# Two products that add to the same PSUM columns, with another block's product between them

## The chip, the cores and the metric

The kernel runs on one core of one Trainium2 chip. The metric is the device time of one execution in microseconds; lower is better. The program is written in Tile: the code says what depends on what, and a scheduler at build time sets the order in which each engine gets its instructions.

## The reference, cut to what matters

A causal attention with a bias from cumulative sums is followed by a gated feed-forward part. B = 8 batches, H = 8 heads, S = 576 tokens, D = 64, 512 model columns, 1024 feed-forward columns, all float32.

```
scores = (q @ k.T) / 8                                  # 64 heads of 576 x 576, causal
cum    = cumsum(max(s, 0)); bias = -(cum[i] - cum[j])
attn   = softmax(where(j > i, -1e9, scores + min(bias, 0)))
x      = (attn @ v), heads side by side                 # [8, 576, 512]
h      = gelu(x @ w_in); u, v = halves of h
v_n    = layernorm(v) * g_ln
v_s    = w_sg @ v_n + b_sg                              # over tokens
out    = x + (u * v_s) @ w_out
```

## The kernel before

All 64 heads go through the same steps: load (L99), split (L264), scores (L323), transposes (L355) and weighted sum (`pv`, L420). The feed-forward part of a batch (`ffn`, L469) is cut into units and strewn between the heads of the next batch, so that TensorE always has something that is ready. Every step has a place on an axis counted in heads (L603 to L646); the code runs through the steps in that order, and the scheduler then reorders instructions on each engine within the limits of the dependences and the buffers.

Float32 precision comes in two ways. Heads 0 to 7 (scores) and 0 to 11 (weighted sum) use plain float32 products, which the trace shows as two records each. All later heads split an operand into a high and a low part (`split`, L83) in the type float32r, and add two products into the same PSUM columns: for the scores, q1 x k1 (L289) and q2 x k2 with 66 rows (L290; the low part of the keys and the bias rows); for the weighted sum, the high and low parts of the transposed probabilities (m[0] and m[1], tiles pah and pal, pbh and pbl, pdh and pdl). These are the split heads of the text: 56 for scores, 52 for the weighted sum.

A head's 576 rows are cut into five blocks of rows: block 0 has 64 rows and 64 columns (causal), blocks 1 to 4 have 128 rows and 192, 320, 448 and 576 columns. [...] The score tiles (`sc`) come from a pool of two buffers. In each product the stationary operand is the block's part of q, 128 columns wide, or 64 for block 0; the moving operand is k, with as many columns as the block. VectorE reads a block out of PSUM with the mask and a running minimum (`ttr`, L292; L297), ScalarE applies exp (L307), GpSimd scales by the reciprocal sums (L321), and TensorE transposes the result (L362, L402).

Before the change `scores` calls `qk_part` for the first block of a tile and then for the second: L289 and L290 of one, then L289 and L290 of the other.

The weighted sum writes a small tile x0 (128 columns, the first token block; L443) and a large tile xx (448 columns, a pool of one buffer), with v as the stationary operand (`mm`, L438). Before the change, x0's two products come first, then a yield (a place where other steps may be put in), then the two products of xx's first 448 columns, and further ones onto parts of them.

The other products of the text are those of the feed-forward part: vm (L494, L508 to L511; 512 columns), um (L556), sm (L571 to L575) and om (L590), all of 288 columns, 12 to 14 in a row onto the same tile.

## Time and profile before

| what | value |
|---|---|
| median of 3 timed runs | 873.3 us (872.01 to 875.57) |
| the profiled execution's span | 869.9 us |
| median less span | 3.4 us |
| instructions in the span | 17259 |
| TensorE busy (products) | 849.2 us, 98% |
| TensorE weight loads busy | 713.6 us, 82% |
| VectorE, ScalarE, GpSimd busy | 671.3, 562.3 and 567.6 us |

The profile is of one execution; its own time is its span, and the timed runs are longer by what lies around it. PE is TensorE's products, PEld its weight loads (they overlap the products), DVE VectorE, ACT ScalarE, POOL GpSimd and SP the engine that issues most transfers. A product's length on the timeline runs from its start to its end through the array, so consecutive ones overlap; the distance between starts tells what one adds. Times in the profile's rows are microseconds.

### The profile page before, as it was taken

The page shows a single profiled execution, that of the slowest core. Times are in us where ns is not written, and L with a number is a line of the kernel's source. Part 1 is how long each engine was busy: PE and PEld are TensorE (multiplying, and loading weights), DVE is VectorE, ACT ScalarE, POOL GpSimd, SP SyncE. Part 2 cuts the span into 40 slices and gives each one's busy share as a digit, 9 for nine tenths or more (in the row PEclk, how much of TensorE's full clock was granted, in tenths as well). Part 3 has the DMA queues.
Part 4 walks back from the last instruction along what each step waited for, and adds up shares of the span by engine and source line. Part 5 has one row for each costly group of instructions (what it writes and reads, how often), then busy time and mean ns, then how long its engine had stood idle before and what let it go on. Part 6 is the DMA issues. An engine that isn't in the chain of part 4 may idle for free.

```text
span 869.9 us, 17259 instructions
## 1 busy us (share of the span) xinstructions
PE 849.2 (98%) x5341; PEld 713.6 (82%) x5341; DVE 671.3 (77%) x2041; ACT 562.3 (65%) x1544; POOL 567.6 (65%) x885
## 2 busy tenths in 40 slices
PE   6899899999999999999999999999999999999988
PEld 3455567988889888898889988889888988899888
DVE  5998778866798678975899668976789668984662
ACT  4677567766687566865677567875668657872340
POOL 4978747767478557685667666786576855773441
PEclk9999999999999999999999999999999999999999
DMA  7556442344333444434424443434344334310101
GB/s 217 173 161 169 125 126 63 104 111 112 86 96 77 107 115 102 106 88 108 125 65 101 112 119 82 98 92 110 105 110 102 87 98 124 77 29 29 40 7 54
DMA packets 68271, 87.23 MB, mean 100 GB/s; under 512 B 24418, under 2 KB 40676, under 8 KB 68180
## 3 DMA queue, kind: packets, MB, share of 16 engines
q1 hardware_dynamic: 68180, 86.14, 37.7%
q8 instruction: 42, 0.69, 0.4%
q14 instruction: 49, 0.40, 0.2%
HBM read 40.17 MB, written 9.73 MB: 57 GB/s over the span
## 4 chain that ended last, share of the span: by engine, by line
PE 89%; DVE 3%; DMA 2%; ACT 2%; POOL 2%; issue 1%; SPq 0%; DVEq 0%; ACTq 0%
PE pt L362 17%; PE om L590 12%; PE xx L438 12%; PE sm L571 11%; PE um L556 10%; PE vm L494 10%; PE sc L289 5%; PE sc L290 5%; PE sc L287 2%; PE x L443 1%; PE sm L574 1%; PE sm L575 1%; PE vm L509 1%; PE vm L508 1%; DMA kf<-in_kq 1%
## 5 line engine op out<-in xcount | busy, mean ns | idle before, releaser
L321 POOL TENSOR_SCALAR p<-p,rs 128x192 f32<-128x192 f32 (+3 forms) x308 | 168.6, 561 | 89.8 <-DVE rs L313 55.3
L307 ACT ACTIVATE p<-p,mn 128x448 f32<-128x448 f32 (+4 forms) x320 | 178.0, 559 | 7.4 <-DVE mn L297 6.9
L362 PE MATMUL pt<-ident,p 128*128 128x128 f32 (+1 forms) x896 | 180.3, 290 | 1.8 <-DVE pah L374 1.6
L297 DVE CUSTOM_DVE_ANT_0 p<-sc,mask 128x448 f32<-128x448 f32 (+4 forms) x320 | 125.5, 422 | 48.3 <-PE pt L362 30.7
L362 PEld LDWEIGHTS pt<-ident,p 128*128 128x128 f32 (+1 forms) x896 | 103.2, 140 | 63.6 <-issue 26.7
L590 PE MATMUL om<-gt,wo 128*128 128x288 f32 x768 | 129.6, 300 | 0.0
L571 PE MATMUL sm<-ws,vn 128*128 128x288 f32 x768 | 124.8, 300 | 1.8 <-DVE u L481 1.2
L556 PE MATMUL um<-xs,wi 128*128 128x288 f32 x768 | 120.8, 298 | 0.3 <-DVE u L577 0.3
L590 PEld LDWEIGHTS om<-gt,wo 128*128 128x128 f32 x768 | 111.5, 188 | 2.6 <-DVE ot L594 0.3
L571 PEld LDWEIGHTS sm<-ws,vn 128*128 128x128 f32 x768 | 108.2, 188 | 3.7 <-DVE u L481 1.9
L90 POOL TENSOR_TENSOR k<-raw,k 128x576 fp32r<-128x576 f32 x56 | 79.8, 1424 | 47.9 <-ACT k L85 44.6
L556 PEld LDWEIGHTS um<-xs,wi 128*128 128x128 f32 x768 | 108.2, 188 | 2.6 <-DVE u L577 0.5
L494 PE MATMUL vm<-wi,xs 128*128 128x512 f32 x384 | 107.8, 401 | 0.5 <-DVE vt L481 0.4
L289 PE MATMUL sc<-k,q 128*128 128x448 f32 x336 | 99.8, 305 | 0.0
L290 PE MATMUL sc<-k,q 66*128 66x448 f32 x336 | 87.8, 296 | 1.0 <-DMA k<-cum 1.0
L90 DVE TENSOR_TENSOR pal<-pt,pah 128x448 fp32r<-128x448 f32 x104 | 63.7, 616 | 19.1 <-ACT pah L85 19.1
L494 PEld LDWEIGHTS vm<-wi,xs 128*128 128x128 f32 x384 | 68.2, 189 | 11.2 <-DVE vt L481 0.7
L90 POOL TENSOR_TENSOR gt<-u,gt 128x288 fp32r<-128x288 f32 x64 | 51.0, 803 | 34.4 <-ACT gt L85 34.4
L85 ACT CAST pah<-pt 128x448 fp32r<-128x448 f32 x104 | 55.1, 532 | 26.7 <-PE pt L362 24.9
L289 PEld LDWEIGHTS sc<-k,q 128*128 128x128 f32 x336 | 60.6, 181 | 10.1 <-DVE wbits L212 1.4
L90 POOL TENSOR_TENSOR vn<-vt,vn 128x512 fp32r<-128x512 f32 x32 | 41.6, 1301 | 40.0 <-ACT vn L85 39.9
L290 PEld LDWEIGHTS sc<-k,q 66*128 66x128 f32 x336 | 60.4, 181 | 6.5 <-DMA k<-cum 1.2
(150 smaller groups left out, 1768.6 us busy)
## 6 DMA issues: line engine op xcount, KB each, us to landing
q<-k SPq DMA_DIRECT2D x168, 144.0 KB
raw<-in_kq SPq DMA_DIRECT2D x56, 288.0 KB
out_t<-ot SPq DMA_DIRECT2D x64, 144.0 KB
vr<-in_vp SPq DMA_DIRECT2D x52, 160.0 KB
k<-k SPq DMA_DIRECT2D x56, 144.0 KB
wraw<-in_w_in SPq DMA_DIRECT2D x16, 256.0 KB
kf<-in_kq SPq DMA_DIRECT2D x8, 288.0 KB
qf<-in_kq SPq DMA_DIRECT2D x8, 288.0 KB
```

The costliest lines, as they stand in the source:

```text
L90: eng_lo.tensor_tensor(out=lo, in0=src, in1=hi.bitcast(F32), op=ALU.subtract)
L289: nc.tensor.matmul(o, d["q1"][:, i0:i0 + r], d["k1"][:, j0:j1], start=True, stop=False)
L290: nc.tensor.matmul(o, q2[h % 2][:, i0:i0 + r], d["k2"][0:66, j0:j1], start=False, stop=True)
L297: nc.vector.tensor_tensor_reduce(out=pbuf[h % 2][it][0:r, j0:j1], in0=pst[0:r, c0:c0 + j1 - j0], in1=mask[0:r, m0 + j0:m0 + j1], scale=-0.125,
L307: nc.scalar.activation(out=p, in_=p, func=AF.Exp, bias=d["mn"][0:r, it:it + 1], scale=-1.0, accum_out=sums[h % 2][0:r, it:it + 1])
L321: e.tensor_scalar(out=p, in0=p, scalar1=rs[0:r, it:it + 1], scalar2=1.0, op0=ALU.mult, op1=ALU.mult)
L362: nc.tensor.transpose(out=ps[:, c:c + r - a], in_=pb[it][a:r, jb:jb + P], identity=ident[a:r, a:r])
L438: nc.tensor.matmul(xx[0:rows, o0:o1], st(jt), m, **{"start": False, "stop": False, **kw})
L494: nc.tensor.matmul(ps[0:r], xs[c][:, xi, ts_], wi[:, c, wj, fs], start=(n == 0), stop=(n == 11))
L556: nc.tensor.matmul(ps[:, 0:CH], wi[:, c, wj, dt * P:(dt + 1) * P], xs[c][:, xi, cs], start=(n == 0), stop=(n == 11))
L571: nc.tensor.matmul(ps[:, 0:CH], vn[j][:, vi, ds_], ws[:, j, wj, cs], start=(n == 0), stop=False)
L590: nc.tensor.matmul(ps[:, 0:CH], wo[:, c, wj, ms], gt[ch, c][:, gi, :], start=(n == 0), stop=(n == 11))
```

## The change

In `scores`, the two blocks that share a tile are handed over together, and the loop over the parts is the outer one: part one of the first block, part one of the second, part two of the first, part two of the second. [...] The tile's last row block (4) is handed over alone, so its pairs stay. In the weighted sum, xx's first product of each part follows x0's of the same part, inside one loop and before the yield. Comment lines are also taken out, which is left out here. In the changed file the score products are lines L292 (part one) and L294 (part two), and later lines are shifted by two or three.

```
-    def qk_part(h, it, pst, c0, j0, j1):
+    def qk_parts(h, pst, *blocks):
+
         d = heads[h]
-        i0, r = IT0[it], ITR[it]
-        o = pst[0:r, c0:c0 + j1 - j0]
-        if h < NQ:
-            nc.tensor.matmul(o, d["q"][:, i0:i0 + r], d["k"][:, j0:j1], start=True, stop=True)
-            return
-        nc.tensor.matmul(o, d["q1"][:, i0:i0 + r], d["k1"][:, j0:j1], start=True, stop=False)
-        nc.tensor.matmul(o, q2[h % 2][:, i0:i0 + r], d["k2"][0:66, j0:j1], start=False, stop=True)
+        for part in range(1 if h < NQ else 2):
+            for n, (it, c0, j0, j1) in enumerate(blocks):
+                i0, r = IT0[it], ITR[it]
+                o = pst[0:r, c0:c0 + j1 - j0]
+                if h < NQ:
+                    nc.tensor.matmul(o, d["q"][:, i0:i0 + r], d["k"][:, j0:j1], start=True, stop=True)
+                elif part == 0:
+                    nc.tensor.matmul(o, d["q1"][:, i0:i0 + r], d["k1"][:, j0:j1], start=(n == 0), stop=False)
+                else:
+                    nc.tensor.matmul(o, q2[h % 2][:, i0:i0 + r], d["k2"][0:66, j0:j1], start=False, stop=True,
+                                     skip_group_check=(n > 0))
...
-        qk_part(h, 3, t, 0, 0, 448)
-        qk_part(h, 0, t, 448, 0, 64)
+        qk_parts(h, t, (3, 0, 0, 448), (0, 448, 0, 64))
...
-        qk_part(h, 2, t, 0, 0, 320)
-        qk_part(h, 1, t, 320, 0, 192)
+        qk_parts(h, t, (2, 0, 0, 320), (1, 320, 0, 192))
...
-        qk_part(h, 4, t, 0, 0, CH)
+        qk_parts(h, t, (4, 0, 0, CH))
...
-        qk_part(h, 4, t, 0, CH, S)
+        qk_parts(h, t, (4, 0, CH, S))
...
         for k in range(parts):
             nc.tensor.matmul(x0[0:rows, 0:P], st(0), m[k][:, 0:P], start=(k == 0), stop=(k == parts - 1))
+            mm(0, 448, 0, m[k][:, P:S], start=(k == 0))
         yield 0.2
-        for k in range(parts):
-            mm(0, 448, 0, m[k][:, P:S], start=(k == 0))
         for k in range(parts):
             mm(128, 448, 2, m[k][:, S:896])
```

On TensorE, around a head's scores and around its weighted sum, this moves the following. Before, at one head's first score tile (sc_4744; k1, q1 and k2, q2 are the parts one and two):

```order
L289 MATMUL sc_4744<-k1_4719,q1_4721 128x448
L290 MATMUL sc_4744<-k2_4720,q2_1_150 128x448
L289 MATMUL sc_4744<-k1_4719,q1_4721 64x64
L290 MATMUL sc_4744<-k2_4720,q2_1_150 64x64
L509 MATMUL vm_4732<-wi_163,xs_4212 64x512
```

After, on TensorE at the same tile:

```order
L513 MATMUL vm_4732<-wi_163,xq_4736 128x512
L292 MATMUL sc_4744<-k1_4719,q1_4721 128x448
L292 MATMUL sc_4744<-k1_4719,q1_4721 64x64
L294 MATMUL sc_4744<-k2_4720,q2_1_150 128x448
L294 MATMUL sc_4744<-k2_4720,q2_1_150 64x64
L558 MATMUL um_4866<-xs_4205,wi_163 128x288 x3
```

The first of the 64-column products, which stood behind the second 448-column product, now stands ahead of it, and other feed-forward work follows the block.

The second place is TensorE's order at one weighted sum (x0_5338 is the small tile, xx_5337 the large one; pah and pal, pbh and pbl are high and low parts of the transposed probabilities). Before:

```order
L443 MATMUL x0_5338<-pah_5305,vs_5259 128x128
L443 MATMUL x0_5338<-pal_5306,vs_5259 128x128
L438 MATMUL xx_5337<-pbl_5322,vs_5259 128x448
L590 MATMUL om_5761<-gt_5571,wo_164 128x288 x2
L438 MATMUL xx_5337<-pdh_5329,vs_5259 128x192
```

After, on TensorE at the same weighted sum:

```order
L592 MATMUL om_5761<-gt_5438,wo_164 128x288 x3
L446 MATMUL x0_5338<-pah_5305,vs_5259 128x128
L446 MATMUL x0_5338<-pal_5306,vs_5259 128x128
L441 MATMUL xx_5337<-pbl_5322,vs_5259 128x448
L592 MATMUL om_5761<-gt_5552,wo_164 128x288
```

Here only the feed-forward work around the pair has moved; x0's two products still follow each other.

## The prediction

> **What bounds the kernel now.** I read the page first, then the windows over equal stretches, then the timeline of TensorE. Here are the span, the engine line of part 1, and three stretches (span time, then each engine's busy time and instructions, then the granted clock and the DMA).

> ```profile
> span 869.9 us, 17259 instructions
> PE 849.2 (98%) x5341; PEld 713.6 (82%) x5341; DVE 671.3 (77%) x2041; ACT 562.3 (65%) x1544; POOL 567.6 (65%) x885
> ...
> 318.00:418.60 100.60, 100.55 (x665) 88.56 (x665) 80.97 (x250) 69.71 (x193) 68.15 (x106) 1.00 0.40 101
> 519.20:619.80 100.60, 100.56 (x666) 88.54 (x665) 80.96 (x250) 69.73 (x193) 68.16 (x106) 1.00 0.40 100
> 821.00:870.00 49.00, 42.56 (x291) 39.42 (x289) 22.87 (x50) 13.83 (x30) 16.44 (x29) 0.99 0.09 29
> ```

> The work repeats every 100.6 us, one batch of eight heads with the feed-forward part of an earlier batch, and TensorE is idle for 0.05 us of it at full clock (1.00). VectorE, the next engine, is 81% busy. So in steady state the time is the sum of what TensorE's instructions take, and only the last 49 us (6.4 idle) and the loading phase have waits that could be had back. Busy time doesn't say what one product costs, because matmuls overlap. I read that from start to start on the timeline (start us, length us, engine, line, operands): the time from one start to the next is what the chain pays.

> **What two products in a row cost.** A head's first score block is here: 448 columns in two parts (L289, L290), then 64 columns in two parts, then other work. The last three rows are the weight loads of the short part; `128*64` is a stationary operand 64 wide.

> ```profile
> 343.89 0.37 PE L289 MATMUL sc<-k,q 128*128 128x448 f32 x1
> 344.09 0.36 PE L290 MATMUL sc<-k,q 66*128 66x448 f32 x1
> 344.30 0.19 PE L289 MATMUL sc<-k,q 128*64 128x64 f32 x1
> 344.33 0.22 PE L290 MATMUL sc<-k,q 66*64 66x64 f32 x1
> 344.38 0.42 PE L509 MATMUL vm<-wi,xs 128*64 128x512 f32 x1
> 344.64 0.39 PE L511 MATMUL vm<-wi,xq 128*128 128x512 f32 x1
> 344.88 0.43 PE L556 MATMUL um<-xs,wi 128*128 128x288 f32 x2
> ...
> 344.30 0.14 PEld L290 LDWEIGHTS sc<-k,q 66*64 66x64 f32 x1
> 344.36 0.14 PEld L509 LDWEIGHTS vm<-wi,xs 128*64 128x64 f32 x1
> 344.42 0.19 PEld L511 LDWEIGHTS vm<-wi,xq 128*128 128x128 f32 x1
> ```

> L289 and L290 add to the same 448 columns; the second starts 0.20 us after the first. The product behind it goes to other columns and starts 0.21 later. So following onto the same columns costs nothing that can be read here. The 288-column blocks say the same (same columns 0.13, another tile 0.14), and behind them stands the weighted sum's first pair, L443:

> ```profile
> 412.33 0.30 PE L289 MATMUL sc<-k,q 128*128 128x288 f32 x1
> 412.46 0.29 PE L290 MATMUL sc<-k,q 66*128 66x288 f32 x1
> 412.60 0.23 PE L443 MATMUL x<-pah,vs 128*128 128x128 f32 x1
> 412.66 0.27 PE L443 MATMUL x<-pal,vs 128*128 128x128 f32 x1
> 412.77 0.42 PE L438 MATMUL xx<-pbl,vs 128*128 128x448 f32 x1
> 413.03 0.42 PE L590 MATMUL om<-gt,wo 128*128 128x288 f32 x2
> ```

> What does cost is a short product, because the load behind it isn't covered. The product that follows then starts on paper but runs late, so I take the stretch up to the start after the next long product and subtract that long one. L443's pair: 413.03 - 412.60 = 0.43, less 0.20 for the 448 columns, is 0.23, so 0.115 for each product of only 128 columns. A lone 192-column product and a pair of them:

> ```profile
> 326.57 0.25 PE L438 MATMUL xx<-pdh,vs 128*128 128x192 f32 x1
> 326.65 0.32 PE L289 MATMUL sc<-k,q 128*128 128x288 f32 x1
> 326.81 0.29 PE L290 MATMUL sc<-k,q 66*128 66x288 f32 x1
> 326.94 0.25 PE L438 MATMUL xx<-pdl,vs 128*128 128x192 f32 x1
> ```

> 326.81 - 326.57 = 0.24, less 0.13 for 288 columns, is 0.11. So a short product followed by a load 128 wide costs 0.11, whether it has 128 or 192 columns: the price is the load's. Now the 64-column pair, in front of the same head's 320-column product this time:

> ```profile
> 333.35 0.20 PE L289 MATMUL sc<-k,q 128*64 128x64 f32 x1
> 333.38 0.22 PE L290 MATMUL sc<-k,q 66*64 66x64 f32 x1
> 333.44 0.39 PE L289 MATMUL sc<-k,q 128*128 128x320 f32 x1
> 333.67 0.31 PE L290 MATMUL sc<-k,q 66*128 66x320 f32 x1
> 333.82 0.26 PE L289 MATMUL sc<-k,q 128*128 128x192 f32 x1
> ```

> 333.67 - 333.35 = 0.32, less 0.15 for 320 columns (333.82 - 333.67), is 0.17 for the pair. Its second product is followed by a load 128 wide, 0.11; that leaves 0.06 for the first, whose follower's load is 64 wide. The rows at 344 agree: there both loads are 64 wide, and the pair costs 344.64 - 344.30 = 0.34, less 0.24 for 512 columns (344.88 - 344.64), so 0.10, twice 0.05.

> **The change part by part.** The same 5341 products and loads run; nothing is added or removed.

> *The 448/64 block.* The first rows of the order shown with the change are those of the timeline at 344 us. The two short products, neighbours before, now each stand in front of a product with a wide load. Before, a 64-wide load followed the first of them; after, the load of the second 448-column product does, 128 wide: 0.11 in place of 0.06, so +0.05. The long products hide the loads behind them as before, and the second 64-column product keeps its 0.11. In the changed order 53 of the 56 split heads have this sequence (in 3, transposes follow): 53 x 0.05 = **+2.65 us**. Bounds: 0 (the load is hidden after all) and 0.11 x 53 = 5.8 (the whole price of a wide load comes on top of the 0.06).

> *The 320/192 block.* Its two short products also stood together:

> ```profile
> 381.52 0.26 PE L289 MATMUL sc<-k,q 128*128 128x192 f32 x1
> 381.61 0.28 PE L290 MATMUL sc<-k,q 66*128 66x192 f32 x1
> 381.72 0.45 PE L590 MATMUL om<-gt,wo 128*128 128x288 f32 x2
> 382.01 0.82 PE L571 MATMUL sm<-ws,vn 128*128 128x288 f32 x5
> ```

> 382.01 - 381.52 = 0.49, less 2 x 0.13 for the two om products, is 0.23: two times 0.115. Apart, each is followed by a 128-wide load as before: 2 x 0.11. **0 us**, within the 0.01 to which the rows are read.

> *Products onto the same columns.* 218 pairs of split-head score products (56 of 448 columns, 54 of 64, 52 of 320, 56 of 192, counted in the order) stood in a row; 0 do now. The last row block of a head, two single pieces of 288, keeps its pairs. The rows above put the wait that this takes away at 0.20 against 0.21 and 0.13 against 0.14: **0 us**. Its bounds are -0.01 and +0.01 a pair, 2.2 us either way.

> *The weighted sum.* The code now puts the large tile's first product between x0's two, but that tile must first be emptied by the head before, and x0's second part comes later from VectorE. In the order shown with the change only the filling work around x0 moved (the rows of before are those at 412 us above); the pair stays together in all 52 split heads. **0 us.**

> *Later results.* Block one's wide part is finished 0.11 later, since a short product stands inside it. VectorE doesn't look at it until long after; this is its read of the block written at 344 us:

> ```profile
> 350.96 0.62 DVE L297 CUSTOM_DVE_ANT_0 p<-sc,mask 128x448 f32<-128x448 f32 x1
> ```

> 6.5 us lie between, so the delay is covered; without that cover it would be 56 x 0.11 = 6.2 us. The list of waits (us in all, times, longest) shows the other direction:

> ```profile
> PEld sc L289 <- DVE mn L297: 1.2, 5, 0.3
> ```

> The first parts of score products waited for VectorE 5 times in the whole run. **0 us.**

> *Waits that the new order makes.* The order of fillers changed everywhere, and no trace of before shows the new one. Downwards, the steady stretches have 0.05 us per batch to give and the last stretch 6.4 us, part of it the last transfer; upwards see the second rival. I take 0, the row nearest to it being the 1.2 us.

> The sum on the profiled execution is 869.9 + 2.65 = 872.55. The three timed runs have a median of 873.3, 3.4 above the profile's span, which I keep: 872.55 + 3.4 = **876.0 us**, 0.3% more. This measurement can tell about 0.5% (4.4 us) from no change.

> **The rivals.**

> *The loads are hidden (no change).* In this one a 128-wide load runs ahead under the long product before the short one, so it doesn't matter which product follows which: 53 x 0 = 0, and 873.3. The timeline speaks against it: 0.11 for 192 columns, 0.115 for 128, where the 64-column pair with narrow loads needs 0.05 each; a load two products ahead would show as less than 0.11. [...]

> *New waits (slower).* Where blocks follow each other with less filler, the second meets a score buffer that VectorE hasn't read. The place is the first product of a score block, behind VectorE's read of the block two before it. It decides where TensorE's work between the two is shorter than VectorE's lag, 6.5 us in the row above. For it: before, the scheduler repeated one order each batch, and after it doesn't. Against it: 1.2 us in 872 so far. If one head in four waits for one read of a wide block, that is 14 x 0.6 = 8.4 us, and 876.0 + 8.4 = 884.4; half of it, 880.2, is the likelier size.

> *The same columns or the edges pay (faster).* If the separated pairs do give their 0.01 each, that is 2.2 us; if the other order also covers half of the last stretch's 6.4 us, 3.2 more: 5.4 in all, and with the short products hidden as in the first rival 873.3 - 5.4 = 867.9; with them paid it is 870.6, within 0.5%. For it: the idle time is there. Against it: nothing in the change works on those waits, and 0.01 is the rows' own resolution.

> *The change doesn't do what it says.* For the weighted sum that is the case, as the order shows, and counted above; for the scores it does.

> **How the numbers follow.** Forecast (short products pay, few waits) 0.47, of it 0.43 within 0.5% and 0.04 slower; loads hidden 0.11, all within; new waits 0.26, all slower; faster side 0.16, of it 0.12 beyond 0.5% and 0.04 within. Together: faster 0.12, same 0.58, slower 0.30. The likeliest case's own range is 873.3 to 879.1 (0 to 5.8 on the short products). For 8 in 10 the range goes down to 869.5, between the faster rival's two ends, and up to 882.0, between the two sizes of the slower one.

> **What would show it.** In the profile of the changed kernel the 64-column product followed by a 448-column one should take 0.11 to the start after next, less the 448's 0.20; a batch should take 100.6 + 8 x 0.05 = 101.0 us, with TensorE still idle for under 0.2 us of it; the 192s should show 0.11 each; x0's pair should be unchanged. I am wrong if the separated pairs start closer than 0.20 (448) or 0.14 (320), if a batch is shorter than 100.6, or if waits of score products for VectorE grow from 1.2 us to more than 3.

## The result, and the profile after

The changed kernel took 903.4 us (median of 4 runs, 901.07 to 903.58), the kernel before 872.65 beside it on the same chip (870.73 to 875.57). The ratio is 1.034, 95% interval 1.031 to 1.037: 3.4% slower, where 0.3% was forecast and 882 was the upper end.

The page of the changed kernel: the span, the engines, and the row of TensorE's clock over 40 equal slices. An 8 or a 7 is a slice of 22.5 us with more than 4.5 us at half speed; a single stretch of 3.4 us still shows as a 9.

```profile
span 901.8 us, 17271 instructions
PE 871.6 (97%) x5341; PEld 724.8 (80%) x5341; DVE 679.8 (75%) x2041; ACT 562.3 (62%) x1544; POOL 565.1 (63%) x885
...
PEclk9899899979999999999999999998999999999999
```

The same 5341 products are busy for 22.4 us more, and the span is 31.9 longer. To see where, I take 130 to 800 us, behind the loading phase and ahead of the last one, first of before, then of after (span time, TensorE's busy time and its products, granted clock):

```profile
130.00:800.00 670.00, 669.65 (x4420) 1.00 0.37 95
```

```profile
130.00:800.00 670.00, 658.05 (x4218) 0.98 0.36 94
```

TensorE now idles for 11.95 us of it instead of 0.35, and its clock has fallen from 1.00 to 0.98. Half speed comes in stretches: five of 3.4 to 10.2 us, 27.3 us together, so 13.7 us are lost. The longest, and what stands ahead of it:

```profile
181.40:184.80 3.40, 2.20 (x13) 1.00 0.23 62
184.80:195.00 10.20, 10.01 (x39) 0.50 0.48 115
```

TensorE idled for 1.20 of 3.40 us, and for the next 10.2 it ran at half speed. Most of the idle time is waiting for VectorE. The first of these rows of the waits (us in all, times, longest) is the one that stood at 1.2 us before: weight loads of score products waiting for VectorE's reads. The other two are the products' own waits:

```profile
PEld sc L292 <- DVE mn L302: 7.5, 11, 1.7
...
PE sc L292 <- DVE mn L302: 5.0, 4, 1.5
PE sm L576 <- DVE vnr L90: 2.7, 2, 1.3
```

These 7.7 us lie in the middle stretch; with smaller rows, 8.7 of its 11.95 us are waits for VectorE, and 1.8 are for ScalarE.

### The profile page after: what moved, and what is told of

Read it like the earlier page. It is cut to its first block, busy times and chain, and to the rows that moved or that the text cites. A ratio compares the mean times of both kernels' runs of the same rounds, so it can differ in the third digit from the quotient of the medians.

```text
span 901.8 us, 17271 instructions
## 1 busy us (share of the span) xinstructions
PE 871.6 (97%) x5341; PEld 724.8 (80%) x5341; DVE 679.8 (75%) x2041; ACT 562.3 (62%) x1544; POOL 565.1 (63%) x885
## 4 chain that ended last, share of the span: by engine, by line
PE 81%; DVE 9%; ACT 4%; issue 2%; DMA 2%; POOL 2%; SPq 0%; DVEq 0%; ACTq 0%
PE pt L365 14%; PE om L592 11%; PE um L558 10%; PE xx L441 10%; PE sm L573 9%; PE vm L496 9%; PE sc L292 4%; PE sc L294 4%; PE sc L290 2%; DVE rs L317 2%; ACT p L312 2%; DVE p L302 1%; PE x L446 1%; PE sm L577 1%; PE sm L576 1%
## 5 line engine op out<-in xcount | busy, mean ns | idle before, releaser
L326 POOL TENSOR_SCALAR p<-p,rs 128x192 f32<-128x192 f32 (+3 forms) x308 | 166.7, 555 | 78.9 <-DVE rs L318 60.2
L312 ACT ACTIVATE p<-p,mn 64x64 f32<-64x64 f32 (+4 forms) x320 | 177.8, 558 | 18.6 <-DVE mn L302 16.2
L302 DVE CUSTOM_DVE_ANT_0 p<-sc,mask 128x448 f32<-128x448 f32 (+4 forms) x320 | 124.5, 423 | 51.6 <-PE pt L365 28.9
L558 PE MATMUL um<-xs,wi 128*128 128x288 f32 x768 | 123.5, 302 | 2.7 <-DVE vt L483 2.1
L592 PE MATMUL om<-gt,wo 128*128 128x288 f32 x768 | 125.6, 299 | 0.1
L573 PEld LDWEIGHTS sm<-ws,vn 128*128 128x128 f32 x768 | 111.4, 194 | 2.2 <-DVE u L483 0.7
L496 PE MATMUL vm<-wi,xs 128*128 128x512 f32 x384 | 104.8, 402 | 0.8 <-DVE ot L596 0.6
L292 PE MATMUL sc<-k,q 128*128 128x448 f32 x336 | 84.7, 307 | 5.2 <-DVE mn L302 5.0
L294 PE MATMUL sc<-k,q 66*128 66x448 f32 x336 | 86.2, 309 | 0.6 <-DMA k<-cum 0.6
L292 PEld LDWEIGHTS sc<-k,q 128*128 128x128 f32 x336 | 54.8, 183 | 15.4 <-DVE mn L302 7.5
L85 ACT CAST pbh<-pt 128x448 fp32r<-128x448 f32 x52 | 27.7, 533 | 55.2 <-PE pt L365 55.1
```

The costliest lines, as they stand in the source:

```text
L292: nc.tensor.matmul(o, d["q1"][:, i0:i0 + r], d["k1"][:, j0:j1], start=(n == 0), stop=False)
L294: nc.tensor.matmul(o, q2[h % 2][:, i0:i0 + r], d["k2"][0:66, j0:j1], start=False, stop=True, skip_group_check=(n > 0))
L302: nc.vector.tensor_tensor_reduce(out=pbuf[h % 2][it][0:r, j0:j1], in0=pst[0:r, c0:c0 + j1 - j0], in1=mask[0:r, m0 + j0:m0 + j1], scale=-0.125,
L312: nc.scalar.activation(out=p, in_=p, func=AF.Exp, bias=d["mn"][0:r, it:it + 1], scale=-1.0, accum_out=sums[h % 2][0:r, it:it + 1])
L326: e.tensor_scalar(out=p, in0=p, scalar1=rs[0:r, it:it + 1], scalar2=1.0, op0=ALU.mult, op1=ALU.mult)
L496: nc.tensor.matmul(ps[0:r], xs[c][:, xi, ts_], wi[:, c, wj, fs], start=(n == 0), stop=(n == 11))
```

## Why VectorE was late

One of these waits followed back. TensorE, around 404 us (start, length, and in brackets the idle time ahead with its releaser):

```profile
403.90 0.75 PE L365 MATMUL pt<-ident,p 128*128 128x128 f32 x4
406.15 0.50 PE L292 MATMUL sc<-k,q 128*128 128x448 f32 x2 [1.51 <-DVE mn L302]
```

A score block waits 1.51 us until VectorE has read the block whose buffer it needs. VectorE's rows there:

```profile
401.16 4.37 DVE L317 TENSOR_SCALAR rs<-sum 128x4 f32<-128x4 f32 x1 [0.41 <-ACT p L312]
405.57 0.18 DVE L318 RECIPROCAL rs<-rs 128x4 f32<-128x4 f32 x1
405.66 0.43 DVE L302 CUSTOM_DVE_ANT_0 p<-sc,mask 128x288 f32<-128x288 f32 x1
```

The read (L302) stands behind rs = sum + 1e-9, an addition on 4 columns. The same operation took 0.16 us at 184.89; here it took 4.37. GpSimd at the time:

```profile
399.85 1.42 POOL L90 TENSOR_TENSOR xs<-xr,xs 128x576 fp32r<-128x576 f32 x1
401.26 0.74 POOL L326 TENSOR_SCALAR p<-p,rs 128x576 f32<-128x576 f32 x1
401.98 1.41 POOL L90 TENSOR_TENSOR xs<-xr,xs 128x576 fp32r<-128x576 f32 x1
403.35 0.80 POOL L90 TENSOR_TENSOR gt<-u,gt 128x288 fp32r<-128x288 f32 x1
404.11 1.40 POOL L90 TENSOR_TENSOR xs<-xr,xs 128x576 fp32r<-128x576 f32 x1
405.94 1.83 POOL L326 TENSOR_SCALAR p<-p,rs 128x448 f32<-128x448 f32 x4 [0.44 <-DVE rs L318]
```

GpSimd worked without a gap until 405.51, then stopped for 0.44 us, and just then VectorE's addition ended (405.53). The same stands at 295.6 us (4.67) and 609.4 us (4.38). So the addition looks like something that waits for a gap in GpSimd's work. Around the wait, TensorE's clock (the windows ahead, of the wait, and behind):

```profile
400.00:403.20 3.20, 3.20 (x25) 3.16 (x25) 2.75 (x6) 1.39 (x6) 3.20 (x3) 1.00 0.00 1
403.20:406.60 3.40, 1.89 (x15) 1.52 (x14) 3.37 (x6) 1.46 (x3) 2.96 (x5) 1.00 0.29 66
406.60:410.00 3.40, 3.40 (x17) 3.00 (x16) 2.63 (x8) 2.17 (x5) 3.40 (x6) 0.52 0.11 25
```

The 1.51 us of waiting are followed by 3.4 us at 0.52, in which 17 products run instead of some 26: the wait is paid a second time.

The theory with which the experiments began: the interleaving itself costs the 2 to 3 us of the forecast; the rest comes from the order that the scheduler chose anew on all engines. The rival: interleaved products are dear in themselves, in a way that the rows of before could not show. The addition was found in the changed kernel's trace after the first four runs; it and the clock were tested in the later ones.

## The experiments

In several kernels the order of every engine is written out, so that an edit changes only what it says. At the end of the program each instruction gets a dependence, without a semaphore, on the one ahead of it in a list:

```diff
         tile_attn_gmlp(tc, *args)
+        pinned(nc, tc)
...
+    for seq in order.values():
...
+        for a, b in zip(seq, seq[1:]):
+            tc.add_manual_dep(made[f"I-{b}"], f"I-{a}", info, reason="pinned")
```

**e1: the interleaving in the old order.** The change's score part, each engine in before's order, the products of a tile interleaved where they stand.

```diff
-        qk_part(h, 3, t, 0, 0, 448)
-        qk_part(h, 0, t, 448, 0, 64)
+        qk_parts(h, t, (3, 0, 0, 448), (0, 448, 0, 64))
...
+        pinned(nc, tc)
```

> Every engine gets its instructions in the order of the kernel before, place by place; only the score blocks of heads 8 to 63 are interleaved as in the change (at the place of the second part of the wide block stands the first part of the narrow one, and the other way round). The weighted sum is as before. Theory (the loss is the new order of everything else, with its waits and the half clock that follows them; the interleaving itself costs only the wide load behind a 64-column product): 872.7 + 53 x 0.05 = 875.4 us, no waits of TensorE in the steady stretches, clock as before (0.995). Rival (the interleaving itself is dear on the chip, about 30 us): 900 to 905 us.

Measured: 874.9 us, before 873.4; ratio 1.0019 (1.0003 to 1.0034). The interleaving costs 0.2%. The block whose rows of before stand in the prediction (343.89 us), in e1, and the block four batches later:

```profile
343.99 0.40 PE L292 MATMUL sc<-k,q 128*128 128x448 f32 x2
344.23 0.48 PE L294 MATMUL sc<-k,q 66*128 66x448 f32 x2
344.55 0.42 PE L512 MATMUL vm<-wi,xs 128*64 128x512 f32 x1
344.81 0.39 PE L514 MATMUL vm<-wi,xq 128*128 128x512 f32 x1
345.04 0.42 PE L559 MATMUL um<-xs,wi 128*128 128x288 f32 x2
...
747.78 0.40 PE L292 MATMUL sc<-k,q 128*128 128x448 f32 x2
```

The later block of before:

```profile
746.36 0.37 PE L289 MATMUL sc<-k,q 128*128 128x448 f32 x1
```

From the block's start to um it is 345.04 - 343.99 = 1.05 us, and 344.88 - 343.89 = 0.99 before: +0.06, where the forecast had +0.05. Four batches take 747.78 - 343.99 = 403.79 against 402.47, so +0.33 a batch of eight heads, where 0.40 was forecast. Over 53 heads that is 2.2 us. The rival falls.

**e2: the new order without the interleaving.** The changed kernel's order on every engine, the four score products of a tile put back side by side.

```diff
-        qk_parts(h, t, (3, 0, 0, 448), (0, 448, 0, 64))
+        qk_part(h, 3, t, 0, 0, 448)
+        qk_part(h, 0, t, 448, 0, 64)
...
+        pinned(nc, tc)
```

> Every engine gets its instructions in the order of the changed kernel, place by place; only the score blocks are put back (both parts of the wide block, then both of the narrow one, on the same four places). Theory (the order costs): 903.4 - 2.7 = about 901 us, with waits of 1.3 to 1.6 us in front of score products and half clock behind them. Rival (the interleaving itself is dear): 870 to 876 us.

Measured: 896.3 us, 5 less than expected and far above the rival's 876; ratio 1.0266 (1.0232 to 1.0299). The order alone costs 23 us.

**e3 and e4: the two halves of the edit, each alone,** with the order left to the scheduler. e3 has only the scores' part, e4 only this:

```diff
             nc.tensor.matmul(x0[0:rows, 0:P], st(0), m[k][:, 0:P], start=(k == 0), stop=(k == parts - 1))
+            mm(0, 448, 0, m[k][:, P:S], start=(k == 0))
         yield 0.2
-        for k in range(parts):
-            mm(0, 448, 0, m[k][:, P:S], start=(k == 0))
```

> Only the score blocks are interleaved; the weighted sum is as before, and the scheduler chooses the order itself. Theory (any edit gives the scheduler another order, whose waits decide): somewhere between 873 and 910 us, in any case the sum of TensorE's products within 3 us of that of before and the rest of the difference in waits and half clock. Rival (one of the two edits carries the loss): 900 to 905 us here and 873 with the weighted sum alone, or the other way round.

> Only the weighted sum's loop is changed; the scores are as before, and the scheduler chooses the order itself. Theory (order luck): between 870 and 900 us, by the waits that the trace then shows. Rival (one of the two edits carries the loss): 873 us if the scores carry it, 900 to 905 us if the weighted sum does.

Measured: e3 899.6 us, ratio 1.0299 (1.0269 to 1.033); e4 872.8 us, ratio 0.9997 (0.9981 to 1.0013). e3 has the order of the changed kernel, instruction for instruction, and e4 that of the kernel before. The weighted sum's part moves nothing at all. So the numbers of the rival came true: the scores' part alone carries the loss. But e1 and e2 show that it does so through the order that it leads to, and not through its products.

**e5 and e6: without the addition,** in the new order and in the old.

```diff
-        nc.vector.tensor_scalar(out=rs[:, c], in0=sums[h % 2][:, c], scalar1=1e-9, scalar2=None, op0=ALU.add)
-        nc.vector.reciprocal(out=rs[:, c], in_=rs[:, c])
+        nc.vector.reciprocal(out=rs[:, c], in_=sums[h % 2][:, c])
```

> The changed kernel with the order of every engine written out as the scheduler chose it, and VectorE's small addition rs = sum + 1e-9 left out (128 of them; the reciprocal reads the sums directly, and a sum is at least 1, so 1e-9 is below its last bit). Theory: in the changed kernel this addition stood for 4.67, 4.37 and 4.38 us at 295.6, 401.2 and 609.4 us of the trace, while GpSimd ran one operation behind the other, and the score products behind it waited 1.02, 1.58 and 1.59 us; behind the two longer waits TensorE's clock was granted at half for 3.4 and 6.8 us. So these three waits go (4.2 us) and with them these two stretches of half clock (half of 10.2, so 5.1 us): about 894, 891 to 896. The waits for vnr at 384 and 592 us and for vt at 182 us stay, with their half clock. Rival one: VectorE is late for another reason and the next operation takes the wait over: 899 to 904, the reciprocal or a two-input operation standing for over 3 us in the addition's place. Rival two: the loss has nothing to do with VectorE: 899 to 904 with the waits gone.

> The kernel before with its own order on every engine written out, and the addition rs = sum + 1e-9 left out in the same way. In the trace of before the addition stood for 1.2 to 2.5 us in 17 places, and TensorE hardly waited there. By the theory that VectorE's late operation only costs where a score product stands close behind it, nothing changes: 871 to 875. If the late addition costs something everywhere, for example through the products that wait a little, some 3 us go: 868 to 870.

Measured: e5 893.1 us (ratio 1.0226, 1.018 to 1.0273), as forecast. VectorE at the place of the 4.37 us, and TensorE's clock there:

```profile
398.83 0.18 DVE L317 RECIPROCAL rs<-sum 128x4 f32<-128x4 f32 x1 [0.41 <-ACT p L312]
400.14 0.46 DVE L302 CUSTOM_DVE_ANT_0 p<-sc,mask 128x288 f32<-128x288 f32 x1 [1.13 <-PE sc L294]
```

```profile
398.00:401.40 3.40, 3.40 (x27) 3.36 (x26) 1.34 (x6) 1.11 (x6) 3.40 (x4) 1.00 0.00 0
401.40:404.80 3.40, 3.40 (x26) 2.84 (x25) 2.30 (x6) 3.38 (x8) 3.40 (x6) 1.00 0.40 88
```

GpSimd is as busy as before (3.40 of 3.40, the fifth pair of columns), but VectorE now waits for TensorE (1.13) and not the other way round; no idle time, no half clock.

e6 was a miss: 877.1 us, ratio 1.0035 (1.0015 to 1.0056), 4 us slower with 128 instructions fewer. (In the trace of before the addition stands for 1.2 us or more in 15 places, not 17.) VectorE came earlier to a later operation, of 64x512 with two inputs from SBUF, in each of five batches; here VectorE, GpSimd and TensorE in the one at 463 us:

```profile
463.31 2.34 DVE L531 SCALAR_TENSOR_TENSOR vt<-vt,mv,g_b 64x512 f32<-64x512 f32 x1
465.58 0.61 DVE L90 TENSOR_TENSOR pal<-pt,pah 128x448 fp32r<-128x448 f32 x1
```

```profile
463.29 0.86 POOL L90 TENSOR_TENSOR vs<-vr,vs 128x320 fp32r<-128x320 f32 x1
464.14 0.22 POOL L525 TENSOR_SCALAR rt<-mv 64x1 f32<-64x1 f32 x1
464.34 0.74 POOL L320 TENSOR_SCALAR p<-p,rs 128x576 f32<-128x576 f32 x1
465.06 1.02 POOL L526 TENSOR_TENSOR rt<-rt,half 64x1 f32<-64x1 f32 x1
```

```profile
466.24 0.27 PE L361 MATMUL pt<-ident,p 64*128 64x64 f32 x1 [0.84 <-DVE pal L90]
```

vt stood through three operations of GpSimd. Then the two change places: GpSimd's second rt (L526), on a single column, stood for 1.02 us while vt ran; the same operation took 0.56 at 260.7 us in the trace of before. pal came late, and TensorE waited 0.84 us; five times that is the 4 us. So the hold isn't a matter of the addition alone: this operation meets it too, and leaving the addition out, which saved time in the new order, costs time in the old one.

**e7: the changed kernel again,** without an edit, beside e5 and e6.

> The changed kernel once more, beside the two others on the same chip, since its own time of 903.4 and the 899.6 of the kernel with the scores alone, whose order of instructions was the same, lie 0.4% apart. Expected 899 to 904.

Measured: 906.4 us (897.38 to 907.67), above the expected 899 to 904; ratio 1.0357 (1.0296 to 1.0418). It scatters more than the kernel before (871.2 to 876.7 there), and the granted clock goes with it: 0.987 in the run of 897.4, 0.973 in that of 907.7. So e3's 899.6 and after's 903.4 lie within what this order does.

**e8: the addition column by column,** in the new order.

```diff
-        nc.vector.tensor_scalar(out=rs[:, c], in0=sums[h % 2][:, c], scalar1=1e-9, scalar2=None, op0=ALU.add)
+        for j in range(c.start, c.stop):
+            nc.vector.tensor_scalar(out=rs[:, j:j + 1], in0=sums[h % 2][:, j:j + 1], scalar1=1e-9, scalar2=None, op0=ALU.add)
```

> The changed kernel with its own order written out on every engine, and the addition rs = sum + 1e-9 kept, but written one column at a time: four operations of 128x1 in the place of one of 128x4. In the trace of the changed kernel the 128x1 additions took 0.15 us at every time, in the middle of GpSimd's work too, and only those of 128x4 stood for up to 4.7 us. Theory: it is the form of the operation that must wait for a gap in GpSimd's work; so at 295, 401 and 609 us the four take some 0.6 us, the three waits of TensorE behind them go as they did with the addition left out, and the time is that of that kernel: 893, 890 to 896. Rival: VectorE stands still there whatever the operation's form (for example it waits for a semaphore of GpSimd that the trace does not show): the first of the four takes over 4 us, 899 to 906.

Measured: 892.9 us, ratio 1.0217 (1.0178 to 1.0256), as forecast. All four additions at the same place:

```profile
394.52 0.34 DVE L318 TENSOR_SCALAR rs<-sum 128x1 f32<-128x1 f32 x4 [0.41 <-ACT p L312]
```

0.34 us for four, against 4.37 for one. It is the form of the operation that is held: 128x4, but not 128x1.

**e9 and e10: the wait of e6 made longer, and taken away.** Old order without the addition; in VectorE's list, in five batches, pal is moved two operations back (e9) or one forward, ahead of vt (e10).

```diff
 vt_4778<-vt_4778,mv_4786,g_b_136 64x512
-pal_4557<-pt_4560,pah_4556 128x448
 u2_4981<-u2_4981,?,um_4968 128x288
 p_0_2_143,mn_4874<-sc_4884,mask_129,?,? 128x320
+pal_4557<-pt_4560,pah_4556 128x448
```

> Old order without the addition (877.1 us, with one wait of TensorE of 0.8 us in each of five batches, none of them followed by half clock), and the operation of VectorE that TensorE waits for there, pal, moved behind two others (u and the read of a score block, some 0.84 us). So the five waits are 1.65 us instead of 0.8: 4.2 us more of idle time. Theory of the clock: where TensorE idles for more than some 1.2 us within one of the fixed stretches of 3.41 us, its clock is at half in the next; the five waits lie at five different places in these stretches, and about three or four of them should fall mainly into one, each costing 1.7 us more: 877 + 4.2 + 5 to 7 = 886 to 888, with three or four stretches of half clock near 365, 466, 568, 670 and 771 us. Rival, the clock falls only after some 3 us of idle time: 881, and no stretch of half clock there.

> The same kernel, old order without the addition, with that pal moved the other way: ahead of vt<-vt,mv,g_b, the operation of 64x512 with two inputs from SBUF that stood for 2.3 us there while GpSimd worked without a gap. Theory: the five waits of 0.8 us go (4 us), vt still stands for 1 to 2 us but nothing stands behind it: 872 to 874, that is the kernel before again. Rival: the 4 us come from elsewhere, or the held operation delays the next reads of VectorE by as much: 876 to 878.

Measured: e10 873.2 us, ratio 0.999 (0.9974 to 1.0007): the 4 us are gone, and the forecast held. e9 883.3 us (882.96 to 887.96), ratio 1.0124 (1.0099 to 1.0149), less than the 886 to 888 expected and more than the rival's 881. All five waits were 1.65 us long, as meant, but only two were followed by half clock. Two of those places and one other, each with the window behind (span time, TensorE busy, granted clock):

```profile
364.30:367.70 3.40, 1.75 (x12) 1.00 0.18 51
367.70:371.10 3.40, 3.40 (x16) 0.51 0.01 2
...
569.10:572.50 3.40, 2.04 (x14) 1.00 0.18 42
572.50:576.00 3.50, 3.21 (x23) 1.00 0.09 32
671.50:674.90 3.40, 1.84 (x13) 1.00 0.39 80
674.90:678.30 3.40, 3.31 (x14) 0.51 0.19 48
```

The half clock starts on a fixed grid of 3.41 us: the changed kernel's five stretches, at 184.86, 386.25, 406.73, 594.46 and 614.94 us, start 59, 6, 55 and 6 steps of 3.413 us apart. Where the whole wait lay within one stretch of the grid (1.65 and 1.56 us idle), the next was at half; where the grid's edge cut it (1.36 and 0.29), it wasn't. The execution shown is one of 888.0 us; in the median, the 877.1 of e6 and 4.2 us of longer waits leave 2.0 for the clock, about one hit of 1.7. I had expected three or four; the threshold is higher, or less sharp, than my 1.2.

**e11: the other waits eased,** in the new order without the addition. At four places TensorE's waiting products or VectorE's held operations are moved behind their neighbours in the lists; one of them, TensorE's:

```diff
 xx_4757<-pah_4726,vs_4671 128x448
-sm_4855<-wr1_166,vnr1_4797 128x288
-sm_5017<-wr1_166,vnr1_4797 128x288
-sm_5125<-wr1_166,vnr1_4797 128x288
 pt_4746<-ident_124,p_1_3_158 128x64
...
 sc_5065<-k2_5005,q2_1_150 128x288
+sm_4855<-wr1_166,vnr1_4797 128x288
+sm_5017<-wr1_166,vnr1_4797 128x288
+sm_5125<-wr1_166,vnr1_4797 128x288
```

> The changed kernel's order without the addition (893.1 us), and at four places the order eased: at 382 and 587 us the six products with wr behind the score products that follow them (PE), and VectorE's vnr behind its pal; at 486 us three products with wr behind two score products; at 183 us VectorE's vt behind the reads of the score block. Theory: waits of 1.35, 0.69, 1.34 and 1.09 us go (4.5 us), and the half clock of 10.2 us at 186 us with the last (5.1 us): 883.5, 881 to 886. What is left above before is then the short product's price of some 3 us, the wait at 179 us and the first 130 us. Rival, the waits move on to the next product that needs VectorE: 888 to 893.

Measured: 889.0 us, ratio 1.0172 (1.0149 to 1.0194): the rival's range, not the theory's 881 to 886. The stretch from 130 to 800 us of e5, then of e11:

```profile
130.00:800.00 670.00, 661.61 (x4298) 0.99 0.37 95
```

```profile
130.00:800.00 670.00, 661.99 (x4320) 1.00 0.37 95
```

The half clock of 10.2 us went, as forecast (one stretch of 3.4 us, at 179 us, is there instead), but the idle time hardly fell (8.39 to 8.01): the waits moved on to other products. This order isn't repaired at four places.

**e12: a gap for VectorE,** in the changed kernel's order with its addition as it is. At the three places GpSimd's operations that need rs are moved ahead, so that it must stop; in GpSimd's list:

```diff
 p_1_4_160<-p_1_4_160,rs_5117,? 128x576
+p_0_3_145<-p_0_3_145,rs_5281,? 128x448
...
 xs_5687<-xr_4198,xs_5687 128x576
 gt_5246<-u2_4676,gt_5246 128x288
 xs_5690<-xr_4645,xs_5690 128x576
-p_0_3_145<-p_0_3_145,rs_5281,? 128x448
```

> The changed kernel with its own order and with the 128x4 addition as it is; on GpSimd alone, at the three places where the addition stood for 4.4 to 4.7 us (295, 401 and 609 us), the four operations p<-p,rs that wait for it are put two or three operations earlier, so that GpSimd must stop and wait for rs there. VectorE's and TensorE's orders stay. Theory, VectorE's addition waits for a gap in GpSimd's work: the gap now comes within 1.5 us, the additions take under 1.5 us there, the three waits of TensorE behind them and their half clock go, and the time is that of the kernel without the addition: 893, 889 to 897. Rival, it is not GpSimd's work that holds the addition: it still takes over 4 us, and the time is 899 to 907.

Measured: 894.3 us, ratio 1.0223 (1.0166 to 1.0281), as forecast. VectorE's addition, then GpSimd's two operations around it:

```profile
393.94 1.22 DVE L317 TENSOR_SCALAR rs<-sum 128x4 f32<-128x4 f32 x1 [0.41 <-ACT p L312]
```

```profile
394.38 0.75 POOL L326 TENSOR_SCALAR p<-p,rs 128x576 f32<-128x576 f32 x1
395.56 1.83 POOL L326 TENSOR_SCALAR p<-p,rs 128x448 f32<-128x448 f32 x4 [0.43 <-DVE rs L318]
```

The addition ended at 395.16, when GpSimd stopped at 395.13. With VectorE's and TensorE's orders untouched, that confirms it: GpSimd's unbroken work is what held it. TensorE's three waits behind the addition are gone from the trace; one of 1.15 us, at 272.8 us, is new.

**e13 and e14: other orders.** The sources of before and of after without the addition, as in e6 and e5, but with the order left to the scheduler, which then chooses others for both.

> The kernel before with the addition left out and the order left to the scheduler, which then chooses another order on every engine (most rows of TensorE's order differ), with the products of before, nothing interleaved. Its twin in before's own order took 877.1. Theory: the loss comes from the order that the scheduler happens to choose, whatever the edit that made it choose anew; before's order is then an uncommonly good one and this one should lose too: 885 to 900, with waits of TensorE for VectorE of 10 us or more and idle time of 25 us or more. Rival: the scheduler finds an order as good as before's wherever products aren't interleaved, and it is the interleaving that leads it to a bad one: 870 to 880.

> The changed kernel with the addition left out and the order left to the scheduler, so that the interleaved products stand in a third order. Its twin in the changed kernel's order took 893.1. Theory, as for the run before it: the time is that of an order drawn anew, 880 to 900, and says nothing of the interleaving. Rival, the interleaving leads the scheduler to a bad order each time: 890 to 900, at least 10 above the run with the old products in another order.

Measured: e13 899.8 us, ratio 1.0302 (1.0273 to 1.0331); e14 895.9 us, ratio 1.0255 (1.0228 to 1.0283). e13 has no interleaved product and is as slow as e3. Its stretch from 130 to 800 us, and its longest wait, on VectorE and on TensorE:

```profile
130.00:800.00 670.00, 654.40 (x4232) 0.99 0.38 96
```

```profile
192.70 4.83 DVE L539 TENSOR_SCALAR vt<-vt,rt 64x512 f32<-64x512 f32 x1
```

```profile
198.12 1.49 PE L361 MATMUL pt<-ident,p 64*128 64x64 f32 x5 [4.57 <-DVE pal L90]
```

15.6 us of idle time, and another operation held, this one of 64x512. So it doesn't take the interleaving to lead the scheduler to a bad order. Three orders chosen anew (after's, e13's, e14's) cost 2.5 to 3.6%, one of them with the old products; it is before's order in which the engines mesh, with 0.35 us of idle time in 670. That is one draw without interleaving, so how often the scheduler hits a good one is open.

No kernel here beats the one before: e4 (872.8, in the order of before), e10 (873.2) and e1 (874.9) come closest.

## Why the prediction was wrong

- *The sum of TensorE's products sets the time.* Right for before, and for the interleaving in before's order. (VectorE's 80.97 us of 100.6 are 80%, not 81.)
- *Products onto the same columns wait for nothing: 0 us.* It stands. Separated in e1, they gave nothing that could be read; e1 is slower by about the next term. (The trace of before has 210 pairs in a row and not 218: inside 8 of those of 448 columns other products stand.)
- *The 64-column product ahead of a wide load: +2.65 us.* Right: 0.06 at one block for 0.05, 0.33 a batch for 0.40, 2.2 us in all, and 1.5 between the medians of e1. The rival, the loads hidden, would have given no difference.
- *The weighted sum: 0 us.* Right (e4, 0.9997).
- *Later results are covered: 0 us.* Right in e1.
- *Waits that the new order makes: I take 0, the nearest row being 1.2 us.* **This step failed.** The waits measured 11.6 us more idle time in the middle stretch, and 13.7 us more were lost there at half clock. Over the whole span, TensorE idles for 9.6 us more than before and loses 20.1 us more to half clock, and its products, counted at full clock, take 2.2 us more: together the 31.9. Some 5 of the 20.1 are from the first 130 us, where the loss scatters from run to run, in before's order too (1.7 us in e1, 8.5 in e6): that part may be chance. Nor need the last 2.2 be the interleaving's, since e2, without it, has 2.0; this count is good to about 1 us (e4, e6, e9 and e10, with before's products in before's order, have -1.3 to 0.3). The 1.2 us was a property of before's order, the very thing that the change replaced, and so no bound for the new one. That the order moved on all engines stood in front of me, and in the rival's "for". Nor was it the nearest row. In the same list other rows bring the waits of L289 for VectorE to 10, 5.2 us in all, and the first eight heads, with plain products in the loading phase, show what such waits can be:

```profile
PEld sc L287 <- DVE mn L297: 8.8, 12, 2.1
```

- *The rival, new waits.* It had the right place, the first product of a score block behind VectorE's read, and the sign I gave (waits for VectorE growing from 1.2 to over 3 us) came: 7.5. Its price, 8.4, was too small: I had put the waits down to blocks that follow each other too closely, and had neither VectorE held for over 4 us nor the clock in it. Its own range should have gone past 900, and its chance above 0.26.

Shown: the order and not the interleaving (e1, e2, e13); the hold of VectorE by GpSimd (e8, e12); the half clock behind long waits (e9, e11). What the hold costs in this order is known only roughly. Without it the times are 892.9 to 894.3 (e5, e8, e12); the order with it took 899.6, 903.4 and 906.4 (e3, the changed kernel, e7), so 5 to 14 us. No run has the new order written out and nothing else changed; the nearest, e2, took 896.3 with the products put back, which speaks for the lower end. Open: why e11 is still 16 us slower than before. Its trace has 9.3 us more idle time, 1.7 more lost to half clock and 4.8 more in the products themselves, counted at full clock, but no run says which neighbours make the products dearer. e13, with no interleaved product, has 6.3 there.

## What to carry to other kernels

Where a scheduler orders the program, an edit that moves nothing important may still have every engine's order drawn anew, and near a full engine the new draw can cost far more than the edit itself (here 23 us against 1.5): write the old order out and try the edit in it before judging the edit. Waits of over a microsecond that appear then may have to be priced twice on TensorE, once as idle time and once as half clock behind it (here 1.51 us, then 3.4 us at 0.52), and followed back through the engine named: the operation that stands long there may itself be held by a third engine (here 4.37 us for an addition that took 0.16 elsewhere).

## What the runs showed of the hardware

*VectorE and GpSimd.* Held by GpSimd's work were an addition of one input on 128x4 (0.14 to 4.67 us in the changed kernel), vt<-vt,rt of 64x512 (0.45 there, 4.83 in e13) and a two-input operation of 64x512 (0.72 in the kernel before, 2.34 in e6); additions on 128x1 (at most 0.16) and the reciprocal on 128x4 (at most 0.18) weren't. Each of the two engines was seen to stand while the other worked: rt's 1.02 us on GpSimd in e6, for 0.56, is the same in the other direction. The hold of VectorE could last over several of GpSimd's instructions in a row, until GpSimd had a gap: the 4.37 us at 401.16 us ran over five of them and ended at 405.53 us, GpSimd's work at 405.51.
